# Gating one matrix's loads out of a shared weight ring, with planning margins, in a recurrent attention and mixer kernel

## The chip, the cores and the metric

The kernel runs on one core of one Trainium2 chip. The metric is the device time of one execution in microseconds (us). The executions of one kernel in one session spread by 7 to 28 us, so nearly every kernel was timed in five rounds beside the kernel before, on the same chip. Each run has one profile, of one of its executions, so differences of a few us between two profiles are noise.

Engines: TensorE (PE in the profile, its weight loads PEld), VectorE (DVE), ScalarE (ACT), GpSimd (POOL), SyncE (SP). SP and POOL both issue DMA transfers here. In the views, `psq`, `psk`, `psv` and `psy` are attention's q, k, v and output products, `psh` and `y` the mixer's (`y` is the one with w4), and `wst` is a slot of the weight ring.

## The reference, cut to what matters

```python
# four layers: attention with recurrent memory, mixer, attention, mixer
x = x + A(layernorm(x)); x = x + B(layernorm(x)); x = x + A(layernorm(x)); x = x + B(layernorm(x))

def A(x, mem0, Wq, Wk, Wv, Wo, seg_len):      # S = 2048, Dm = 640, 32 heads of 192, segments of 32
    mem = mem0                                # 8 memory rows
    for s in range(64):
        h = concat([mem, x[segment s]])       # 40 rows
        q, k, v = h @ Wq, h @ Wk, h @ Wv      # each 640 x 6144
        o = softmax(mask(q k^T) * scale) v @ Wo
        mem = o[:8]; outs.append(o[8:])       # the next segment needs this segment's memory rows

def B(x, w1, w2, w3, w4):                     # w1, w2: 640 x 640; w3: 640 x 1536; w4: 1536 x 640
    h = gelu(layernorm(x) @ w1); x1 = x + shift(h) @ w2
    return x1 + gelu(layernorm(x1) @ w3) @ w4
```

(Keyword details, the mask and the shift are left out.)

The recurrence makes attention a chain of 64 segments. Each one needs all of Wq, Wk, Wv and Wo again, 31 MB, not all of which is kept on the chip.

## The kernel before

Both attention layers run at once as two lanes, the second five segments behind the first, so that one pass over the weights serves both (80 columns in a full step, 40 where only one lane runs). There are 69 steps (48 us long in the model, eight groups of heads). After every second step a mixer chunk of 128 rows is worked off beside the next two steps.

About 60% of the attention weights stay resident. The rest comes through a ring of 16 slots, which the mixer's weights share. SP issues attention's loads, POOL the mixer's. Each queue is sorted by a "due" time and issued in that order. Cuts are marked by `...`:

```python
RING = 16; RING_A = 14; RING_B = 5         # slots; most that attention / the mixer may hold
...
plan = Plan({**PSUM_BANKS, "r": RING}, {**PSUM_USES, "ra": ("r", RING_A), "rb": ("r", RING_B)})
...
def block(t, kind, g, c, due):             # one streamed block of an attention weight
    ...
    b = ring("ra")
    def fn(op):
        return nc.sync.dma_start(out=T(b)[:, 0:n], in_=w_src(kind, g, c, c + 1)[:, 0, :])
    add("SP", SP_US, due, fn, w=(b,), dma=P * n * 2, queue="wa")
...
def load_b(c, nm, n, due):                 # one block of a mixer weight
    ...
    b = ring("rb")
    ...
    add("SP" if B_SP else "POOL", SP_US if B_SP else POOL_US, due, fn, w=(b,), dma=P * wd * 2, queue="wb")
```

A small simulator inside the kernel (`Plan.place`) plays all operations through a model of the engines and of the transfers, before the program is built. What it yields is the order of the instructions on each engine. At run time every engine works through its instructions in that order. If data come later than the model thought, the engine stands (below, TensorE for 1.24 us at one such place), whatever stands further down its list.

```python
if o.dma:
    srv = max(s + DMA_LAT, srv) + o.dma / DMA_RATE    # when the model thinks the data are there
    done = srv + DMA_SKEW
...
    b.free_at = max(b.free_at, done + LAT)            # when the slot can be filled again
...
for x in o.succ:
    if o.dma:
        at = done                                     # when the reader may be placed
```

In a step (48 us long in the model, eight groups of heads), `v` of the last group is due at 45.6, and the output weights of all groups are held back to the step's end, from 44 on:

```python
proj_v(g + 1, base + sl * (g + 1.6))        # last group: base + 6 * 7.6 = base + 45.6
...
held = g >= NG - OT_BUFS + 1                # true for all groups here
at = base + STEP - HOLD + 0.5 * g if held else ...     # HOLD = 4: base + 44, 44.5, 45, 45.5, 46, ...
ws = [block(t, "o", g, c, at + 0.03 * c) for c in range(GC)]
```

Of the kernel before, what the change touches and what calls it, by code (L numbers as in the profile page):

```python
# [20 lines left out]
LAG = 5  # L21
HG = 4
RING = 16
RING_A = 14
RING_B = 5
B_SP = False
POOL_US = 0.9
SP_US = 0.47
CUT = {"k": [3] * 8, "q": [3] * 8, "v": [3] * 8, "o": [2] + [4] * 7}
YA = 3  # L30
STEP = 48.0
# [10 lines left out]
LAT = 0.2  # L42
# [3 lines left out]
DMA_LAT = 2.2  # L46
DMA_SKEW = 2.0
FLIGHT = 10


class Buf:
# [34 lines left out]
class Plan:  # L86
# [48 lines left out]
    def place(self):  # L135
        in_queue = {}
        head = {}
        for q, lst in self.queues.items():
            lst.sort(key=lambda o: (o.due, o.i))
            for k, o in enumerate(lst):  # L140
                in_queue[o.i] = (q, k)
            head[q] = 0
        engines = sorted({o.e for o in self.ops})
        cand = {e: [] for e in engines}
        free = dict.fromkeys(engines, 0.0)
        waiting = {}

        def offer(o):
            if o.i in in_queue:
                q, k = in_queue[o.i]  # L150
                if k != head[q]:
                    waiting[o.i] = o
                    return
            cand[o.e].append(o)

        for o in self.ops:
            if o.n == 0:
                offer(o)
        left = len(self.ops)
        srv = 0.0  # L160
        landed = []
        out = []

        def est(o, t):
            s = max(t, o.ready)
            if o.dma and o.e == "SP" and len(landed) >= FLIGHT:
                s = max(s, landed[-FLIGHT])
            need = {}
            for b in o.slots:
                if b.slot is None:  # L170
                    need[b.cls] = need.get(b.cls, 0) + 1
            for c, n in need.items():
                fs = self.free_slots[self.pool_of[c]]
                al = self.allowed[c]
                if len(fs) < n or len(al) < n:
                    return None
                s = max(s, fs[n - 1][0], al[n - 1])
            return s

        while left:  # L180
            best = None
            for e in engines:
                t = free[e]
                lst = cand[e]
                if not lst:
                    continue
                vals = []
                m = None
                for o in lst:
                    s = est(o, t)  # L190
                    if s is not None:
                        vals.append((s, o))
                        if m is None or s < m:
                            m = s
                if m is None:
                    continue
                if best is not None and m >= best[0]:
                    continue
                lim = m + (LOOK if e == "PE" else 0.05)
                s, o = min((so for so in vals if so[0] <= lim), key=lambda so: (so[1].due, so[1].i))  # L200
                if best is None or s < best[0]:
                    best = (s, o)
            assert best is not None, "no operation can be placed"
            s, o = best
            e = o.e
            for b in o.slots:
                if b.slot is None:
                    b.slot = self.free_slots[self.pool_of[b.cls]].pop(0)[1]
                    self.allowed[b.cls].pop(0)
            o.start = s  # L210
            o.end = s + o.d
            free[e] = o.end
            done = o.end
            if o.dma:
                srv = max(s + DMA_LAT, srv) + o.dma / DMA_RATE
                done = srv + DMA_SKEW
                if e == "SP":
                    landed.append(done)
            cand[e].remove(o)
            out.append(o)  # L220
            left -= 1
            for b in o.slots:
                b.left -= 1
                b.free_at = max(b.free_at, done + LAT)
                if b.left == 0:
                    bisect.insort(self.free_slots[self.pool_of[b.cls]], (b.free_at, b.slot))
                    bisect.insort(self.allowed[b.cls], b.free_at)
            for x in o.succ:
                if o.dma:
                    at = done  # L230
                elif x.e == e:
                    at = o.end
                else:
                    at = o.end + (PE_LAT if e == "PE" else LAT)
                if at > x.ready:
                    x.ready = at
                x.n -= 1
                if x.n == 0:
                    offer(x)
            if o.i in in_queue:  # L240
                q, k = in_queue[o.i]
                head[q] = k + 1
                lst = self.queues[q]
                if k + 1 < len(lst) and lst[k + 1].i in waiting:
                    x = waiting.pop(lst[k + 1].i)
                    cand[x.e].append(x)
        return out
# [3 lines left out]
def kernel(  # L251
# [16 lines left out]
    nc = tc.nc  # L268
    P = 128
# [191 lines left out]
            return Dm, w4_v[:, n, :]  # L461
        return Dm, B_w2[P * n:P * n + P, :]

    def load_b(c, nm, n, due):

        if c >= NCH - 2:
            return ahead[nm, n]
        b = ring("rb")
        wd, src = mixer_src(nm, n)

        def fn(op):
            return (nc.sync if B_SP else nc.gpsimd).dma_start(out=T(b)[:, 0:wd], in_=src)  # L472
        add("SP" if B_SP else "POOL", SP_US if B_SP else POOL_US, due, fn, w=(b,), dma=P * wd * 2, queue="wb")
        return b, lambda: T(b)[:, 0:wd]


# [6 lines left out]
        return r  # L483

    last = [()]

    def HX(t, kc):
        return [B("hT", t % 4, k) for k in ("x0", "mA" if kc < YA else "mB", "xa", "xb", "xc")]

    def attention_step(t):  # L490
# [11 lines left out]
        def proj_kq(g, s0):  # L502
            G = t * NG + g
            for kind, off in (("k", 0.0), ("q", 0.3 * sl)):
                pq = ps("P", [P, GC, NS], f32, "ps" + kind)
                now = []
                for kc in range(KC):
# [7 lines left out]
                                             start=pq.begin(), stop=True, skip_group_check=True)  # L515
                    now.append(add("PE", mm_us(N, k=GC), due, fn, r=(wb, *HX(t, kc)), a=(pq,), after=last[0]))
                last[0] = now
                if kind == "q":
                    q = qT[G % 2]

                    def fq(op, pq=pq, q=q):
                        nc.scalar.copy(out=q[:, :, 0:N], in_=T(pq)[:, :, 0:N])  # L522
                    add("ACT", act_us(GC * N), s0 + off, fq, r=(pq,), w=(B("qT", G % 2),))
                else:
                    k_ = kT[G % 2]

                    def fk(op, pq=pq, k_=k_):
                        p4 = T(pq)[:].rearrange("p (h c) n -> p h c n", h=2)
                        k4 = k_[:].rearrange("p (h c) n -> p h c n", h=2)
                        nc.vector.tensor_copy(out=k4[:, :, 0::3, 0:N], in_=p4[:, :, 0::2, 0:N])  # L530
                    add("DVE", dve_us(4 * N), s0 + off, fk, r=(pq,), w=(B("kT", G % 2, 0),))

                    def fk2(op, pq=pq, k_=k_):
                        p4 = T(pq)[:].rearrange("p (h c) n -> p h c n", h=2)
                        k4 = k_[:].rearrange("p (h c) n -> p h c n", h=2)
                        for hf in range(2):
                            nc.vector.tensor_tensor(out=k4[:, hf, 1:3, 0:N],
                                                    in0=p4[:, hf, 1:2, 0:N].to_broadcast([P, 2, N]),
                                                    in1=halves[:].unsqueeze(2).to_broadcast([P, 2, N]), op=ALU.mult)
                    add("DVE", 2 * dve_us(2 * N), s0 + off, fk2, r=(pq,), w=(B("kT", G % 2, 1),))  # L540
# [297 lines left out]
    def prefetch(c):  # L838

        base = (2 * c + 2) * STEP  # L840
        units = [(nm, n, w[0] + w[1] * n) for nm, k, w in (("w1", KC, W1), ("w2", KC, W2), ("w3", 2 * KC, W3), ("w4", FC, W4))
                 for n in range(k)]
        for i, (nm, n, at) in enumerate(units):
            b, tl = resident["kqv"[i // 3 % 3], i // 9]
            wd, src = mixer_src(nm, n)
            ub = Buf()

            def fn(op, tl=tl, i=i, wd=wd, src=src):
                return nc.gpsimd.dma_start(out=tl[:, i % 3, 0:wd], in_=src)
            add("POOL", POOL_US, base + at * 0.6 * STEP, fn, w=(ub,), a=(b,), dma=P * wd * 2, queue="wb")  # L850
            ahead[nm, n] = ub, lambda tl=tl, i=i, wd=wd: tl[:, i % 3, 0:wd]

    def x2_chunks(a, b):
# [3 lines left out]
    def chunk(c):  # L857
# [102 lines left out]
        pz = [ps("B", [P, 3, XB], f32, "psh") for _ in range(2)]  # L960
        for kc in range(KC):
            due = D(W1[0] + W1[1] * kc)
            wb, wv = load_b(c, "w1", kc, due)

            def fw(op, kc=kc, wv=wv, pz=pz):
                w = wv()
# [150 lines left out]
    for t in range(T_A):  # L1117
# [3 lines left out]
        attention_step(t)  # L1121
        for _ in mixer:
            pass
        if c is not None:
            chunk_end(c)
    for c in range((T_A - 2 + 1) // 2, NCH):
        for _ in chunk(c):
            pass
        chunk_end(c)
    placed = plan.place()  # L1130
    ctx.enter_context(tc.manual_schedule())
    flight = []
# [43 lines left out]
```

## Time and profile before

| | before |
|---|---|
| median of three runs | 3533.4 us (3530.5 to 3536.1) |
| TensorE busy, weight loads busy | 96%, 92% |
| transfers | 1089 MB, 308 GB/s |
| a steady pair of steps, mean of 30 | 100.1 us |
| first step, and last step with the last chunk | about 99 us, 88.5 us |

The second line says that there is little room: TensorE is nearly always busy.

### The profile page before, as it was taken

How to read it: one execution, taken by the hardware profiler on the slowest of the kernel's cores; microseconds unless marked ns; L12 is line 12 of the kernel's file. 1: busy time of each engine (PE TensorE's matmuls, PEld its weight loads, DVE VectorE, ACT ScalarE, POOL GpSimd, SP SyncE). 2: the span in 40 equal slices, each digit the busy share in tenths (PEclk: the TensorE clock that was granted, in tenths of full speed). 3: DMA queues.
4: the chain of work that ended last, by engine and by line, in shares of the span. 5: the costliest groups of instructions: out<-in, count | busy, mean ns of one | idle time of the engine just before them, and what ended most of it. 6: DMA issues, size and time to landing. Idle time of an engine off the chain costs nothing.

```text
span 3534.4 us, 194661 instructions
## 1 busy us (share of the span) xinstructions
PE 3384.3 (96%) x84693; PEld 3257.0 (92%) x84693; DVE 2378.1 (67%) x7184; ACT 1714.3 (49%) x3583; POOL 883.9 (25%) x1581
## 2 busy tenths in 40 slices
PE   6899999999999999999999999999999999999897
PEld 4789999999999999999999999999999999999786
DVE  2456777777666777676677776766667777766455
ACT  2334555545554555454445554545455554554343
POOL 1022222222222222222222222222222222222222
PEclk9999999999999999999999999999999999999898
DMA  9999999999999999999999999999999999999995
GB/s 339 308 304 312 311 314 311 312 309 316 311 314 310 312 309 307 315 304 311 301 314 310 306 315 309 308 305 313 308 310 324 310 313 308 313 309 313 298 317 193
DMA packets 735258, 1089.24 MB, mean 308 GB/s; under 512 B 95358, under 2 KB 691596, under 8 KB 734400
## 3 DMA queue, kind: packets, MB, share of 16 engines
q1 hardware_dynamic: 669504, 874.19, 75.5%
q0 software_dynamic: 64896, 202.59, 17.1%
q8 instruction: 662, 10.85, 1.3%
q14 instruction: 196, 1.61, 0.1%
HBM read 1071.16 MB, written 5.24 MB: 305 GB/s over the span
## 4 chain that ended last, share of the span: by engine, by line
PE 80%; DMA 14%; issue 4%; DVE 1%; POOL 1%; ACT 0%; SPq 0%; POOLq 0%; DVEq 0%; ACTq 0%
PE psy L653 15%; PE psq L514 14%; PE psv L555 14%; PE psk L514 14%; DMA wst<-in_B_w_dram 5%; PE psvt L567 5%; PE pss L586 4%; PE pso L634 4%; PE psh L1025 3%; DMA wst<-in_A_Wv_dram 3%; DMA wst<-in_A_Wo_dram 2%; PE y L1047 2%; PE pst L619 2%; PE hs L994 1%; PE psh L968 1%
## 5 line engine op out<-in xcount | busy, mean ns | idle before, releaser
L472 POOL DMA_DIRECT2D wst<-in_B_w_dram x1056 | 581.7, 551 | 1690.5 <-PE psy L653 387.9
L640 DVE CAST oT<-pso 128x480 bf16<-128x480 f32 (+1 forms) x552 | 342.3, 620 | 413.6 <-PE pso L634 412.6
L571 ACT COPY V<-psvt 80x768 bf16<-80x768 bf16 (+1 forms) x552 | 439.3, 796 | 332.1 <-PE psvt L567 323.5
L514 PEld LDWEIGHTS <-wst 128*128 128x128 bf16 x13248 | 555.6, 100 | 31.2 <-issue 10.2
L653 PE MATMUL psy<-oT,wo 128*128 128x80 bf16 (+1 forms) x10350 | 511.0, 199 | 21.1 <-DMA wo<-in_A_Wo_dram 9.1
L522 ACT CAST qT<-psq 128x480 bf16<-128x480 f32 (+1 forms) x552 | 292.5, 530 | 441.7 <-PE psq L514 364.2
L555 PE MATMUL psv<-hT,wv 128*128 128x80 bf16 (+1 forms) x9936 | 477.8, 199 | 6.2 <-issue 3.5
L514 PE MATMUL psk<-hT,wk 128*128 128x80 bf16 (+1 forms) x9936 | 465.0, 199 | 5.6 <-issue 4.2
L514 PE MATMUL psq<-hT,wq 128*128 128x80 bf16 (+1 forms) x9936 | 454.7, 199 | 12.4 <-DMA wq<-in_A_Wq_dram 7.1
L561 ACT CAST vTs<-psv 128x480 bf16<-128x480 f32 (+1 forms) x552 | 292.1, 529 | 335.0 <-PE psv L555 325.0
L653 PEld LDWEIGHTS <-wo 128*128 128x128 bf16 x10350 | 423.0, 99 | 28.3 <-issue 12.5
L597 DVE CUSTOM_DVE_ANT_1 pss<-pss,mask 80x320 f32<-80x320 f32 (+1 forms) x512 | 245.8, 480 | 270.3 <-PE pss L586 228.5
L555 PEld LDWEIGHTS <-wv 128*128 128x128 bf16 x9936 | 405.3, 99 | 20.2 <-issue 4.3
L514 PEld LDWEIGHTS <-wk 128*128 128x128 bf16 x9936 | 399.7, 100 | 14.4 <-issue 6.5
L514 PEld LDWEIGHTS <-wq 128*128 128x128 bf16 x9936 | 393.6, 100 | 20.8 <-DMA wq<-in_A_Wq_dram 8.1
L514 PE MATMUL psk<-hT,wst 128*128 128x80 bf16 (+1 forms) x6624 | 352.9, 199 | 8.6 <-issue 8.0
L653 PE MATMUL psy<-oT,wst 128*128 128x80 bf16 (+1 forms) x6210 | 351.8, 199 | 8.8 <-DMA wst<-in_A_Wo_dram 4.7
L555 PE MATMUL psv<-hT,wst 128*128 128x80 bf16 (+1 forms) x6624 | 342.6, 199 | 12.4 <-DMA wst<-in_A_Wv_dram 9.2
L624 ACT COPY PT<-pst 80x320 bf16<-80x320 bf16 (+1 forms) x552 | 223.0, 404 | 261.6 <-PE pst L619 258.8
L514 PE MATMUL psq<-hT,wst 128*128 128x80 bf16 (+1 forms) x6624 | 326.2, 199 | 8.3 <-DMA wst<-in_A_Wq_dram 5.2
L604 ACT ACTIVATE pss<-pss,sm 80x320 f32<-80x320 f32 (+1 forms) x552 | 261.4, 474 | 137.4 <-DVE sm L597 137.3
L609 DVE TENSOR_REDUCE sm<-pss 80x4 f32<-80x320 f32 (+1 forms) x552 | 251.9, 456 | 92.5 <-ACT pss L604 91.7
(135 smaller groups left out, 5501.6 us busy)
## 6 DMA issues: line engine op xcount, KB each, us to landing
wst<-in_A_Wk_dram SPq DMA_DIRECT2D x1104, 192.0 KB, 4.7
wst<-in_A_Wq_dram SPq DMA_DIRECT2D x1104, 192.0 KB, 4.7
wst<-in_A_Wv_dram SPq DMA_DIRECT2D x1104, 192.0 KB, 4.8
wst<-in_A_Wo_dram SPq DMA_DIRECT2D x1242, 160.0 KB, 4.7
wst<-in_B_w_dram POOLq DMA_DIRECT2D x726, 160.0 KB, 5.0
wst<-in_B_w_dram POOLq DMA_DIRECT2D x330, 192.0 KB, 5.3
wk<-in_A_Wk_dram SPq DMA_DIRECT2D x8, 576.0 KB, 7.6
wq<-in_A_Wq_dram SPq DMA_DIRECT2D x8, 576.0 KB, 7.4
```

The source lines that it names most:

```text
L472: return (nc.sync if B_SP else nc.gpsimd).dma_start(out=T(b)[:, 0:wd], in_=src)
L514: nc.tensor.matmul(out=o[:, c, 0:N], lhsT=w[:, c * P:(c + 1) * P], rhs=h[:, kc, c0:c0 + N], start=pq.begin(), stop=True, skip_group_check= ...
L522: nc.scalar.copy(out=q[:, :, 0:N], in_=T(pq)[:, :, 0:N])
L555: nc.tensor.matmul(out=o[:, c, 0:N], lhsT=w[:, c * P:(c + 1) * P], rhs=h[:, kc, c0:c0 + N], start=pv.begin(), stop=True, skip_group_check= ...
L561: nc.scalar.copy(out=vs[:, :, 0:N], in_=T(pv)[:, :, 0:N])
L571: nc.scalar.copy(out=V_[0:N, :, 0:Dh], in_=T(pt)[0:N].rearrange("n c f -> n (c f)").rearrange("n (i e) -> n i e", i=HG))
L597: nc.vector.tensor_tensor_reduce(out=o, in0=o, in1=maskt.unsqueeze(1).to_broadcast([N, HG, N]), scale=-scale, scalar=3.0e38, op0=ALU.add, ...
L604: nc.scalar.activation(out=o, in_=o, func=ACT.Exp, bias=sm_[0:N, 0:1], scale=-1.0)
L609: nc.vector.reduce_sum(out=sm_[0:N, 4:4 + HG], in_=o, axis=AX.X)
L624: nc.scalar.copy(out=Pt[0:N, :, 0:N], in_=T(pst)[0:N, :, 0:N])
L640: nc.vector.tensor_copy(out=o_[:, :, 0:N], in_=T(pso)[:, :, 0:N])
L653: nc.tensor.matmul(out=T(psy[j])[:, m - m0, c0:c0 + N], lhsT=w[:, m * P:(m + 1) * P], rhs=o_[:, c, 0:N], start=psy[j].begin(), stop=True, ...
```

## The change

The intent: the five blocks of the mixer's first matrix (w1) shall not sit in the ring for half a pair before they are read; they wait for the end of the step ahead, and attention may use all 16 slots meanwhile. The plan gets margins for the mixer's loads. The weights of the last two chunks, which are loaded once and shared, go into SP's queue, in one order with attention's.

```diff
-RING_A = 14
+RING_A = 16
+B_SLACK = 1.5
+AH = 8.0
+B_FREE = 0.5
...
-                b.free_at = max(b.free_at, done + LAT)
+                b.free_at = max(b.free_at, done + (B_FREE if b.cls == "rb" else LAT))
...
-                    at = done
+                    at = done + (B_SLACK if o.e == "POOL" else 0.0)
...
+                mark[t, g] = now[:1]              # first matmul of group g's q in step t
...
-            wb, wv = load_b(c, "w1", kc, due)
+            wb, wv = load_b(c, "w1", kc, due, mark.get((2 * c + 1, NG - 1), ()))
...                                               # shared load of the last two chunks
-                return nc.gpsimd.dma_start(out=tl[:, i % 3, 0:wd], in_=src)
-            add("POOL", POOL_US, base + at * 0.6 * STEP, fn, w=(ub,), a=(b,), ..., queue="wb")
+                return nc.sync.dma_start(out=tl[:, i % 3, 0:wd], in_=src)
+            add("SP", SP_US, base + at * 0.6 * STEP + AH, fn, w=(ub,), a=(b,), ..., queue="wa")
```

(`load_b` passes the new argument on as `after`. Also, `chunk_end` is added to the plan one step later.)

More of the change, by code (lines that the diff above doesn't have):

```diff
@@ L462, in mixer_src, with load_b @@
         return Dm, B_w2[P * n:P * n + P, :]
-    def load_b(c, nm, n, due):
+    def load_b(c, nm, n, due, after=()):
         if c >= NCH - 2:
@@ L472, in fn @@
             return (nc.sync if B_SP else nc.gpsimd).dma_start(out=T(b)[:, 0:wd], in_=src)
-        add("SP" if B_SP else "POOL", SP_US if B_SP else POOL_US, due, fn, w=(b,), dma=P * wd * 2, queue="wb")
+        add("SP" if B_SP else "POOL", SP_US if B_SP else POOL_US, due, fn, w=(b,), dma=P * wd * 2, queue="wb", after=after)
         return b, lambda: T(b)[:, 0:wd]
@@ L485 @@
     last = [()]
+    mark = {}
     def HX(t, kc):
@@ L848, in fn @@
             def fn(op, tl=tl, i=i, wd=wd, src=src):
-                return nc.gpsimd.dma_start(out=tl[:, i % 3, 0:wd], in_=src)
-            add("POOL", POOL_US, base + at * 0.6 * STEP, fn, w=(ub,), a=(b,), dma=P * wd * 2, queue="wb")
+                return nc.sync.dma_start(out=tl[:, i % 3, 0:wd], in_=src)
+            add("SP", SP_US, base + at * 0.6 * STEP + AH, fn, w=(ub,), a=(b,), dma=P * wd * 2, queue="wa")
             ahead[nm, n] = ub, lambda tl=tl, i=i, wd=wd: tl[:, i % 3, 0:wd]
@@ L1123 @@
             pass
-        if c is not None:
-            chunk_end(c)
-    for c in range((T_A - 2 + 1) // 2, NCH):
-        for _ in chunk(c):
-            pass
-        chunk_end(c)
+        if t >= 3 and t % 2 == 1:
+            chunk_end((t - 3) // 2)
+    chunk_end(NCH - 2)
+    for _ in chunk(NCH - 1):
+        pass
+    chunk_end(NCH - 1)
     placed = plan.place()
```

## The prediction

> **What bounds the kernel now.** I read the page first, then the chain of waits, then busy time by stretch, the waits of TensorE, and last the timeline of the loads. From the page: the busy row of TensorE, two rows of the forty slices, and the head of the chain.
>
> ```profile
> PE 3384.3 (96%) x84693; PEld 3257.0 (92%) x84693; DVE 2378.1 (67%) x7184; ACT 1714.3 (49%) x3583; POOL 883.9 (25%) x1581
> ...
> PEclk9999999999999999999999999999999999999898
> ...
> GB/s 339 308 304 312 311 314 311 312 309 316 311 314 310 312 309 307 315 304 311 301 314 310 306 315 309 308 305 313 308 310 324 310 313 308 313 309 313 298 317 193
> ...
> PE 80%; DMA 14%; issue 4%; DVE 1%; POOL 1%; ACT 0%; SPq 0%; POOLq 0%; DVEq 0%; ACTq 0%
> ```
>
> TensorE is busy 96% of the span, weight loads 92%, and four fifths of the chain is TensorE: it is the first suspect. The rate of transfer is a flat 310 GB/s, which could be a second roof. Two stretches of the start, one steady pair of attention steps and the last step of the recurrence tell the two apart (columns: stretch, its length, busy time and count of each engine, granted clock, DMA share, GB/s).
>
> ```profile
> 20.00:60.00 40.00, 29.95 (x574) 23.88 (x575) 10.70 (x45) 10.88 (x26) 0.00 (x0) 1.00 1.07 373
> 100.00:140.00 40.00, 37.82 (x1157) 34.39 (x1154) 17.48 (x74) 17.47 (x42) 0.00 (x0) 1.00 0.94 303
> 1544.00:1644.00 100.00, 98.22 (x2458) 96.03 (x2455) 71.11 (x209) 51.20 (x104) 25.89 (x46) 1.00 0.95 309
> 3446.00:3504.00 58.00, 51.60 (x1270) 44.67 (x1266) 34.52 (x123) 22.48 (x55) 23.23 (x42) 0.88 0.88 293
> ```
>
> The first stretch shows that 373 GB/s is to be had. So 303 to 309 is not the transfer roof; it is what a ring of 16 slots gives when each slot waits for its reader, is filled, and waits again. For TensorE's own floor in a pair I take three entries of the chain:
>
> ```profile
> 1526.64 1.07 PE psq L514 x30
> ...
> 1555.54 0.84 PE psh L968 x15
> ...
> 1567.31 1.09 PE hs L994 x8
> ```
>
> That is 36 ns a matmul of 80 columns, 56 ns of 128 and 136 ns of 320. By the code one full step has 1056 matmuls of 80 columns (720 for q, k and v, 240 for the output, 64 and 32 in attention), 38 us; 48 transposes of 128 columns, 2.7; and 48 score matmuls at some 50 ns, 2.4. Two steps are 86 us. A mixer chunk adds 115 of 56 ns (6.4) and 34 of 136 ns (4.6). The pair's floor is 97 us, and it takes 100: only about 3% is left in a steady pair. At the edges, where only one lane runs, a step is well above its floor.
>
> **What the Trainium skill says.** "Perfetto Trace Analysis", section Optimization Strategy, says that consistent bubbles on an engine that should be saturated can mean that there is too little buffer for the next tile. The trace agrees in kind, but the steady bubbles are small (below). "DMA: Bandwidth & Descriptors", section Issuing engines are not separate DMA queues, says that transfers from all issuers share the same 16 engines and interleave, so that another issuer saves only issue time. The trace shows what that could save here: an issue by POOL takes 0.55 us, one by SP 0.33 to 0.38, and neither queue is full. The same page's Specifications give about 358 GB/s from HBM for a core; 373 was measured here, and the measurement decides. "TensorE: Matmul & The Clock Gate", section on the clock gate, has half rate after idle windows; the page's clock row stays at 9 until the last slices, and the pair above has 1.00, so in the steady part little is to be won there.
>
> **The change part by part.**
>
> 1. The first mixer weights (5 loads) wait for the first q matmul of the last group of the step ahead. Here is when they were issued before, and when they are first read; the first line is the last load of the preceding matrix:
>
> ```profile
> 1519.40 0.55 POOL L472 DMA_DIRECT2D wst<-in_B_w_dram  x1 [0.95 <-PE psq L514]
> 1521.17 0.55 POOL L472 DMA_DIRECT2D wst<-in_B_w_dram  x1 [1.23 <-DMA wst<-in_B_w_dram]
> 1522.52 0.55 POOL L472 DMA_DIRECT2D wst<-in_B_w_dram  x1 [0.80 <-PE y L1047]
> 1523.43 0.55 POOL L472 DMA_DIRECT2D wst<-in_B_w_dram  x1 [0.37 <-PE psk L514]
> 1524.84 0.55 POOL L472 DMA_DIRECT2D wst<-in_B_w_dram  x1 [0.86 <-PE psq L514]
> ...
> 1528.87 0.60 POOL L472 DMA_DIRECT2D wst<-in_B_w_dram  x1 [1.40 <-PE psv L555]
> ```
>
> They are read at 1554.8 to 1557. Their slots are thus held about 30 us of every 100. But the new gate opens at 1526.64 (the x30 of q above is the last group's). Four loads move by some 2 to 5.5 us, the fifth not at all: 15 slot-us out of the ring's 1600 per pair. A landing takes 5 us, so the loads are still there 20 us early. In a steady pair this part is nearly nothing, because the gate opens only when the old schedule had almost finished these loads.
>
> 2. In the start it is more. The first five were issued at 7 to 11 us, and POOL's next load of the ring is at 154 us: five slots lay full and unread through steps 0 and 1. Their 0.8 MB go out of the stretch that runs at 373 GB/s (2.2 us). Step 1 (99 to 142 us, 12.4 MB by the code, which at 303 GB/s is 41 us) ran with 11 slots. With 16 it could go toward 12.4 MB / 0.373 = 33 us; TensorE needs about 31 (25 ns for a matmul of 40 columns, x30 in 0.75 us in the chain). I take 5 us for both, as the w1 loads come back at the end of step 1.
>
> 3. RING_A from 14 to 16 matters only when the mixer holds fewer than two slots. It asks greedily and holds up to five in a steady pair, so attention has 11 and the old cap was hardly ever reached. Worth: 0 to 3 us in all, mainly between the last w4 read and the gate, and in the last step.
>
> 4. The margins: the plan, which fixes each engine's order, counts a POOL load as landed 1.5 us later, and a mixer slot as free 0.5 instead of 0.2 us after its reader. The rows they concern, from TensorE's waits between 250 and 3250 us (total, times, longest):
>
> ```profile
> PE y L1047 <- DMA wst<-in_B_w_dram: 14.6, 23, 1.9
> ...
> PE psy L653 <- DMA wst<-in_A_Wo_dram: 4.3, 8, 1.1
> PE psv L555 <- DMA wst<-in_A_Wv_dram: 1.5, 4, 0.6
> PE psq L514 <- DMA wst<-in_A_Wq_dram: 1.0, 2, 0.7
> ```
>
> The y waits are 23 of 0.6 us mean, longest 1.9, so a margin of 1.5 should cover most: 11 of the 14.6 us. The ring waits of attention sum to 6.8 us in the same stretch; parts 1 and 3 may take 2 of them.
>
> 5. The 32 shared loads of the last two chunks go from POOL to the SP queue, in one order with attention's, 8 us later. Attention should win and the mixer lose in 3446 to 3504; the bytes are the same. Step 68 ends at 3504 and the 30 us chain after it does not change. I take 2 us, between a gain of 8 and a loss of 5.
>
> 6. chunk_end is added to the plan a step later: the same dues, the same predecessors, only another tie-break. Nothing by itself.
>
> Sum: 5 + 2 + 11 + 2 + 2 = 22 us; 3533 - 22 = 3511 us.
>
> **The rivals.** First, that ring slots are the real limit and the freed ones let transfers go at 373 instead of 309 GB/s everywhere. For it: the rate. Against it: the steady pair is 3 us above its floor, so even perfect feeding gives 3 x 31 pairs, about 90 us, and the slots move by only 5 us in 100. It would give 3450 to 3480. Second, that the margins cost more than they save. Five slots with a cycle near 7 us (12 w4 loads in 17 us) would be planned at 8.8 us, the mixer would finish about 3 us later in the pair, and the normalised rows for the next step with it. Against it: y ends at 1524.6 and the next step starts near 1542, with only the short chain of normalisation between. It would give 3535 to 3560. Third, that the SP queue, served in order, holds attention's loads behind a shared load that waits for a resident tile's last reader: 5 to 10 us at the end, 3515 to 3525. Fourth, that the changed order of the whole plan is a fresh draw: pairs of one and the same plan take from 97.4 to 103.7 us, so a few us either way are luck.
>
> **Range and chances.** The gain is made of small terms that are each bounded by a row above, and a new plan may shift other waits by 10 to 15 us. Predicted 3511 us, 3488 to 3535 with 8 in 10. Over 2% faster means under 3464 us, 69 us less: this needs the first rival, 0.05. Over 2% slower means above 3605: 0.01. Within 2%: 0.94.
>
> **What would show it.** Right: no POOL load of the ring before about 125 us; step 1 shorter by 4 to 6 us and its rate above 330 GB/s; the wait of y on mixer weights under 5 us in total; the five w1 loads issued a few us later than before, in a burst after the last group's q; steady pairs near 99.5 us. Wrong: a steady rate well above 320 GB/s with pairs near 97 (first rival); y or the state copies later and a new wait of k or q at the step's start (second); SP waits on TensorE's last readers near 3450 us with attention starved (third).

## More of the kernel before

One view was not looked at closely enough when the prediction was written. It is the timeline of SP's loads at the end of an odd step (columns: start, length, engine, line, operation, names, count):

```profile
1519.35 0.80 SPq L448 DMA_DIRECT2D wst<-in_A_Wv_dram  x2
1521.33 7.00 SPq L448 DMA_DIRECT2D wst<-in_A_Wo_dram  x10
1528.82 2.12 SPq L448 DMA_DIRECT2D wst<-in_A_Wv_dram  x2
1531.03 5.15 SPq L448 DMA_DIRECT2D wst<-in_A_Wo_dram  x8
```

Here is the queue order. Ten output blocks take 7 us to issue (SP waits for a slot's last reader before seven of them, 5.6 us in all by its waits in 1521 to 1528.5), and only then come the last group's v blocks, although v is used before most of the output weights.

(The program also lets SP have at most ten transfers in flight. That did not hold SP up: wherever the traces tell the landings, 3820 loads (95 to 3400 us), the tenth load back had landed before SP's previous issue ended.)

## The result, and the profile after

The changed kernel took 3529.3 us (median of four runs, 3524.0 to 3534.0), against 3534.7 for the kernel before. The ratio was 0.9985, with a 95% interval of 0.9963 to 1.0007. A ratio is the mean time of one kernel's fast runs over the mean of the other's in the same rounds, so it is not quite the ratio of the medians. Repeated later in five rounds, it was 0.9964 (0.9948 to 0.9980; 3526.5 us). So the change is worth some 5 us, not clear of zero, by the first measurement and 12 by the second. "Within 2%" held and so did the range, but the predicted 22 us were not there.

From the page after:

```profile
PE 3372.2 (96%) x84693; PEld 3247.2 (92%) x84693; DVE 2372.7 (67%) x7184; ACT 1715.8 (49%) x3583; POOL 857.8 (24%) x1549
...
GB/s 339 312 320 312 313 301 316 315 307 314 315 313 315 314 314 308 308 310 309 315 314 315 301 309 319 306 317 312 312 311 319 308 318 306 311 315 315 319 308 162
```

The rate is as flat as before; no 373 GB/s appears beyond the start. The first rival is out. (The chain of waits can't be compared: in the trace after it breaks off at the end, with 0% everywhere.)

TensorE's waits in the window from 250 to 3230 us (who waited for what, total us, times, longest), first before, then after:

```profile
PE y L1047 <- DMA wst<-in_B_w_dram: 14.6, 23, 1.9
...
PE psv L555 <- DMA wst<-in_A_Wv_dram: 1.1, 3, 0.6
```

```profile
PE psv L560 <- DMA wst<-in_A_Wv_dram: 20.8, 28, 1.6
...
PE psq L518 <- DMA wst<-in_A_Wq_dram: 0.7, 1, 0.7
PE psy L658 <- DMA wst<-in_A_Wo_dram: 0.6, 2, 0.3
PE psvt L572 <- issue: 0.4, 2, 0.2
...
PE y L1052 <- issue: 0.2, 1, 0.2
```

This is the first finding. The wait of y on mixer weights, 14.6 us before, has gone entirely. In its place the wait of v on its streamed blocks has grown from 1.1 us to 20.8 us. It sits in one place of a step: 20 of the 28 waits come 88 to 91 us after the start of a pair, the other 8 about 40 us after it, in the even step. It is the v of a step's last group. SP's loads there:

```profile
1612.38 1.32 SPq L451 DMA_DIRECT2D wst<-in_A_Wv_dram  x2
1614.37 6.60 SPq L451 DMA_DIRECT2D wst<-in_A_Wo_dram  x10
1621.06 0.86 SPq L451 DMA_DIRECT2D wst<-in_A_Wv_dram  x2
1622.01 6.28 SPq L451 DMA_DIRECT2D wst<-in_A_Wo_dram  x8
```

The ten output blocks still take 6.6 us, with 16 slots allowed (3.0 us of it are waits for slots' readers), and TensorE's timeline at the same place shows what it waits for:

```profile
1624.59 0.46 PE L591 MATMUL pss<-kT,qT 128*80 128x80 bf16 x6
1626.28 0.39 PE L560 MATMUL psv<-hT,wst 128*128 128x80 bf16 x6 [1.24 <-DMA wst<-in_A_Wv_dram]
```

It stands for 1.24 us until the block issued behind the ten has landed.

The start was the second place. The same two stretches as in the prediction, after:

```profile
20.00:60.00 40.00, 28.95 (x557) 23.11 (x554) 10.55 (x45) 10.47 (x25) 0.00 (x0) 1.00 1.07 372
100.00:140.00 40.00, 36.87 (x1080) 32.78 (x1077) 16.70 (x71) 16.63 (x41) 2.77 (x5) 0.99 0.94 304
```

```profile
122.24 0.60 POOL L475 DMA_DIRECT2D wst<-in_B_w_dram  x1 [113.79 <-DMA wst<-in_A_Wk_dram]
```

The gate works as foreseen: POOL's first ring load comes at 122 us. But step 1 runs at 304 GB/s, as before, with five more slots, so these did not raise the rate. SP still waits for the readers of slots there (12.4 us of the 22 from 100 to 122, 9.1 before).

The end was the third. The last step of attention, and the last chunk after it, before and then after:

```profile
3445.90:3504.20 58.30, 51.75 (x1275) 44.84 (x1272) 34.70 (x124) 22.48 (x55) 23.33 (x42) 0.88 0.88 292
3504.20:3534.40 30.20, 13.46 (x134) 9.64 (x134) 14.37 (x45) 5.42 (x14) 2.50 (x3) 0.72 0.01 2
```

```profile
3426.40:3485.90 59.50, 53.33 (x1272) 45.13 (x1269) 33.89 (x122) 22.24 (x55) 5.02 (x9) 0.89 0.90 283
3485.90:3523.00 37.10, 13.75 (x136) 9.89 (x133) 15.16 (x46) 5.41 (x14) 3.01 (x4) 0.66 0.01 4
```

The last chunk has the same work, yet takes 6.9 us longer. The closing instructions of POOL (shortest, median and longest in ns) tell why; the kernel before comes first:

```profile
L1171 POOLq DRAIN  x3: 46/93/2716, 3530.9 to 3534.1; - x3
```

```profile
L1176 POOLq DRAIN  x3: 46/93/9069, 3513.1 to 3522.7; - x3
```

The last store was issued at 3513.1 us in the changed kernel and landed at 3515.0; POOL's DRAIN ran on to 3522.2.

Put together from the starts of the chunks in the two profiled runs (one run each, so a few us are noise):

| stretch | before | after | difference |
|---|---|---|---|
| to the first chunk | 141.7 | 142.1 | +0.4 |
| first pair, one lane | 102.7 | 98.5 | -4.2 |
| 30 pairs | 3003.3 | 2990.9 | -12.4 |
| next pair, one lane from there on | 104.3 | 98.0 | -6.3 |
| next pair | 93.9 | 96.9 | +3.0 |
| last step | 58.2 | 59.5 | +1.3 |
| last chunk to the end | 30.3 | 37.1 | +6.8 |
| span | 3534.4 | 3523.0 | -11.4 |

### The profile page after: what moved, and what is told of

Its sections match the earlier page's. It is cut to its first block, busy times and chain, and to the rows that moved or that the text cites. A ratio compares the mean times of both kernels' runs of the same rounds, so it can differ in the third digit from the quotient of the medians.

```text
span 3523.0 us, 194519 instructions
## 1 busy us (share of the span) xinstructions
PE 3372.2 (96%) x84693; PEld 3247.2 (92%) x84693; DVE 2372.7 (67%) x7184; ACT 1715.8 (49%) x3583; POOL 857.8 (24%) x1549
## 5 line engine op out<-in xcount | busy, mean ns | idle before, releaser
L475 POOL DMA_DIRECT2D wst<-in_B_w_dram x1056 | 574.3, 544 | 1991.1 <-PE psh L1030 631.0
L518 PEld LDWEIGHTS <-wst 128*128 128x128 bf16 x13248 | 550.7, 100 | 27.7 <-issue 7.2
L658 PE MATMUL psy<-oT,wo 128*128 128x80 bf16 (+1 forms) x10350 | 498.8, 199 | 13.6 <-DMA wo<-in_A_Wo_dram 7.7
L518 PE MATMUL psq<-hT,wq 128*128 128x80 bf16 (+1 forms) x9936 | 463.4, 199 | 15.3 <-DMA wq<-in_A_Wq_dram 9.4
L560 PE MATMUL psv<-hT,wv 128*128 128x80 bf16 (+1 forms) x9936 | 468.9, 199 | 6.5 <-issue 3.3
L560 PEld LDWEIGHTS <-wv 128*128 128x128 bf16 x9936 | 397.4, 99 | 15.4 <-issue 4.8
L518 PE MATMUL psk<-hT,wst 128*128 128x80 bf16 (+1 forms) x6624 | 343.7, 199 | 6.9 <-issue 3.9
L560 PEld LDWEIGHTS <-wst 128*128 128x128 bf16 x6624 | 279.4, 99 | 38.0 <-DMA wst<-in_A_Wv_dram 32.6
```

The source lines that it names most:

```text
L475: return (nc.sync if B_SP else nc.gpsimd).dma_start(out=T(b)[:, 0:wd], in_=src)
L518: nc.tensor.matmul(out=o[:, c, 0:N], lhsT=w[:, c * P:(c + 1) * P], rhs=h[:, kc, c0:c0 + N], start=pq.begin(), stop=True, skip_group_check= ...
L560: nc.tensor.matmul(out=o[:, c, 0:N], lhsT=w[:, c * P:(c + 1) * P], rhs=h[:, kc, c0:c0 + N], start=pv.begin(), stop=True, skip_group_check= ...
L658: nc.tensor.matmul(out=T(psy[j])[:, m - m0, c0:c0 + N], lhsT=w[:, m * P:(m + 1) * P], rhs=o_[:, c, 0:N], start=psy[j].begin(), stop=True, ...
```

## The experiments

All kernels gave correct results. The theories: A, the new wait of v comes from the order and pace of the loads at a step's end and shows as soon as y's wait is gone; B, the gate makes it, because w1's five loads now fall into that very place. C came later: the plan is too hopeful about attention's loads. The four parts of this section ran in the same rounds; the changed kernel itself was not in them.

### One part at a time

**The margins alone** on the kernel before.

```diff
+B_SLACK = 1.5
+B_FREE = 0.5
```

> The kernel before with the two planning margins alone (POOL loads counted 1.5 us later, mixer slots free after 0.5 us). Theory A (the waits of y move to the last group's v, because the loads of the step's end arrive no earlier): TensorE's wait of y on mixer weights, 14.6 us before, falls under 2 us, its wait of psv on the v weights rises from 1.5 to over 8 us in the steady part, and the time stays within 10 us of before (ratio 0.997 to 1.000). Theory B (the gate makes the wait of v): y's wait goes, psv's stays under 4 us, and the time falls by 12 us or more (ratio under 0.9965).

Measured: 3516.5 us, ratio 0.9958 (0.9938 to 0.9979), 14 us in the means. The y row is gone:

```profile
PE psv L557 <- DMA wst<-in_A_Wv_dram: 6.0, 12, 2.1
...
PE psy L655 <- DMA wst<-in_A_Wo_dram: 5.3, 10, 1.2
```

Alone, this part won at least as much as the whole change (5 and 12 us). The wait of v grew by 5 us, less than A said, and the time fell by more. The prediction's 11 us for this part were about right.

**The gate and RING_A 16** on the kernel before.

```diff
-RING_A = 14
+RING_A = 16
+... mark.get((2 * c + 1, NG - 1), ())
```

> The kernel before with the gate on the first mixer weights and RING_A 16, without the margins and with the shared load as before. Theory A: y's wait stays near 14 us, psv's wait stays under 8 us, ratio 0.998 to 1.001. Theory B: psv's wait on v weights comes to 15 us or more although y's is still there, so the kernel is no faster or slower than before (1.000 to 1.004). In both the start gains under 3 us, as the w1 loads come back at the end of step 1.

Measured: 3536.7 us, ratio 1.0013 (0.9989 to 1.0037): nothing, or slightly slower.

```profile
PE y L1049 <- DMA wst<-in_B_w_dram: 10.6, 21, 1.2
...
PE psv L557 <- DMA wst<-in_A_Wv_dram: 7.1, 10, 1.8
```

So both parts bring on the wait of v, and neither theory has it right alone: 6.0 us with the margins, 7.1 with gate and ring, 20.8 with all.

**The shared load alone** on SP, on the kernel before.

> The kernel before with the shared load alone on the SP queue, 8 us later. If the loss of the end seen in the changed kernel's profile (the last two stages 88.5 to 96.6 us) is due to this part: the time from the transposes of the last but one chunk to the end is 3 to 9 us above 88.5, the rest as before, ratio 1.001 to 1.0025. If it is due to the new plan in general: within 2 us of 88.5 and a ratio of 1.000.

Measured: 3546.5 us, ratio 1.0038 (1.0015 to 1.0061), 14 us slower. The last step and chunk took 60.4 and 37.1 us, 9 more than the 88.5 before, and POOL's last DRAIN 8.8 us. This part costs, and more than expected.

**The changed kernel without the gate.**

```diff
-            wb, wv = load_b(c, "w1", kc, due, mark.get((2 * c + 1, NG - 1), ()))
+            wb, wv = load_b(c, "w1", kc, due)
```

> The changed kernel without the gate (RING_A 16, margins, shared load kept). Theory A: psv's wait on v weights stays above 10 us in the steady part, time within 5 us of the changed kernel (ratio to before 0.997 to 1.000). Theory B: the wait falls under 5 us and the kernel is 10 us or more faster than the changed one (ratio under 0.9965).

Measured: 3520.5 us, ratio 0.9961 (0.9938 to 0.9984), v waiting 13.0 us. As A said, the wait stays. The changed kernel has 0.9985 and 0.9964 in other rounds, so within the intervals the gate is worth nothing in it.

Where v's loads and v's matmuls meet, taken from the traces as medians of the pairs (us after the start of the pair, odd steps; the landing is known in about half of the pairs):

| kernel | v loads issued | second landed | second block used | wait of v |
|---|---|---|---|---|
| before | 85.5 | 91.1 | 92.5 | 1.1 |
| margins alone | 85.1 | 91.0 | 91.2 | 6.0 |
| gate and RING_A 16 | 83.5 | 88.8 | 88.7 | 7.1 |
| changed | 83.5 | 89.5 | 89.4 | 20.8 |

The gate does help attention: its v blocks land some 2 us earlier. But the plan, which knows of the freed slots, puts their use 3 to 4 us earlier, right onto the landing. The margins do the same from the other side: v is used 1.3 us earlier, while its blocks land as late as before. (The 1.1 us of before is for the window to 3230 us; the prediction's 1.5 is to 3250.)

### The queue order, and three rivals of it

**The last group's v blocks ahead of the output blocks**, nothing else, on the changed kernel:

```diff
-                wb, wv = block(t, "v", g, kc, due)
+                wb, wv = block(t, "v", g, kc, due - (2.0 if g == NG - 1 else 0.0))
```

> The changed kernel with one due changed: the v weights of a step's last group stand in the load queue ahead of the ten output weights, no longer behind them. Theory A (queue order and the rate of the load stream at the step's end set the new wait): the second v load of the odd step lands 5 us or more earlier than 89.5 us after the pair's start, psv's wait on v weights in the steady part falls from 20.8 to under 5 us, psy's wait on output weights rises to 3 to 15 us, and the time falls by 0 to 12 us against the changed kernel. Theory C (the plan's order on TensorE is too hopeful about attention's loads, whichever comes last): the wait moves whole to psy, the sum stays 15 us or more, no gain.

Measured: 3509.2 us, ratio 0.9909 (0.9890 to 0.9929). SP's queue now reads

```profile
1613.03 3.17 SPq L451 DMA_DIRECT2D wst<-in_A_Wv_dram  x4
1616.29 11.13 SPq L451 DMA_DIRECT2D wst<-in_A_Wo_dram  x18
```

and TensorE's waits

```profile
PE psy L658 <- DMA wst<-in_A_Wo_dram: 5.2, 6, 1.8
```

with 0.6 us for v. The second v block lands at 82.6 instead of 89.5. It is the strongest single edit: the three other variants of the changed kernel in these rounds have means of 3527.5 to 3528.3 us, this one 3508.2, so 19 us, more than the 12 that had been the upper end. The changed kernel itself was not in these rounds.

**A margin of 0.8 us on SP's loads too** (theory C), on the changed kernel.

```diff
+A_SLACK = 0.8
...
-                    at = done + (B_SLACK if o.e == "POOL" else 0.0)
+                    at = done + (B_SLACK if o.e == "POOL" else A_SLACK)
```

> The changed kernel with a planning margin of 0.8 us on the SP loads too. Theory C: the sum of TensorE's waits on ring loads of attention falls from 22 to under 8 us in the steady part and the kernel gains 8 to 15 us on the changed one. Theory A: the loads arrive no earlier, TensorE meets them in another order, and the waits stay above 12 us.

Measured: 3526.8 us, ratio 0.9966 (0.9945 to 0.9987). The waits fell to 8.2 us, almost as C said:

```profile
PE psv L561 <- DMA wst<-in_A_Wv_dram: 4.5, 7, 0.9
PE psy L659 <- DMA wst<-in_A_Wo_dram: 3.1, 4, 1.2
```

but the time did not, as far as other rounds tell: the changed kernel has 0.9964 in its own repeat. The second v block lands at 89.7 us, no earlier than in the changed kernel. Here a wait that was planned away was not time won.

**A later gate**, at the last output matmul of the step ahead, on the changed kernel.

```diff
-mark.get((2 * c + 1, NG - 1), ())
+mark.get((2 * c + 1, "o"), ())
```

(The new mark is set where that matmul is added to the plan.)

> The changed kernel with the gate of the first mixer weights at the last output matmul of the step ahead, so that attention has all 16 slots through the step's end. If the five slots and the transfers of those loads are what delays attention there: the last output load is issued 1 us or more earlier than 90.3 us after the pair's start, ring waits of attention fall under 10 us in the steady part, 5 to 15 us faster than the changed kernel. If the loads at the next step's start only shift: psk, psq or psh L9xx waits of 5 us or more appear and the time stays.

Measured: 3529.8 us, ratio 0.9973 (0.9950 to 0.9995). The last output block is issued at 89.1 instead of 90.3 and v waits 11.6 us instead of 20.8, but there is no gain beyond the spread.

**The very last store issued by SP**, on the changed kernel, to see what the DRAIN hangs on.

```diff
-                nc.gpsimd.dma_start(out=dst[w0 + a:w0 + b, :], in_=xo[2 * a + lane:2 * b:2, :])
+                return (nc.sync if c == NCH - 1 else nc.gpsimd).dma_start(...)
...
```

(In the plan this store counts for SP accordingly.)

> The changed kernel with only the very last store issued by SP instead of POOL. The three kernels with the shared load on SP ended with a DRAIN of POOL of 8.8 to 9.1 us after its last store, those without with 2.7 us. If the drain follows POOL's last transfer: it now starts before the last chunk is done, is hidden, and the last stage falls from 37.1 to 30 to 31 us, ratio 0.0015 to 0.002 lower than the changed kernel's. If it is due to something else at the end: the last stage stays above 36 us.

Measured: 3526.4 us, ratio 0.9964 (0.9941 to 0.9987). The DRAIN is as long as ever, 9.6 us, but starts at 3507.4 us and ends before the kernel does:

```profile
L1176 POOLq DRAIN  x3: 46/98/9577, 3507.4 to 3523.3; - x3
```

The last chunk takes 30.9 us. So 6 of the 14 us of the shared load on SP are this DRAIN at the very end. In the ratio 6 us are too few to be seen.

### Putting parts together

The next four ran in the same rounds. **The changed kernel again:**

> The changed kernel itself once more, in the same rounds as the next three, so that they can be set against it: ratio to before 0.996 to 1.000, the wait of psv on v weights 12 to 25 us in the steady part, POOL's last DRAIN near 9 us.

Measured: 3526.5 us, ratio 0.9964 (0.9948 to 0.9980), v waiting 24.5 us, DRAIN 9.1 us.

**The changed kernel with v ahead and the shared load back on POOL:**

> The changed kernel with the last group's v loads ahead of the output weights and with the shared load back on POOL's queue. If the parts add: the 0.9909 of the run with the v loads ahead, less the 6 to 13 us that the shared load on SP cost alone: 0.987 to 0.9905, with POOL's last DRAIN back at 2.7 us. If the SP order of the shared load helped the last step of attention: 0.991 or more.

Measured: 3503.1 us, ratio 0.9894 (0.9877 to 0.9912), DRAIN 2.7 us.

**With v ahead and the last store on SP, the shared load left on SP:**

> The changed kernel with the v loads ahead and the last store on SP; the shared load stays on SP. If only the drain made the shared load on SP costly: as fast as the run before this or faster, 0.987 to 0.990, last stage near 31 us. If the later mixer in the last step costs as well: 2 to 6 us slower than the run before this.

Measured: 3503.5 us, ratio 0.9898 (0.9882 to 0.9914). The two are equal; once the drain is hidden, the issuer of the shared load no longer shows.

**The kernel before with the margins and v ahead**, without gate, RING_A 16 and shared load on SP:

> The kernel before with the margins and the v loads ahead, without gate, RING_A 16 and shared load on SP. If gate and RING_A 16 give attention something once the queue order is right: 4 us or more slower than the run with the v loads ahead and the shared load on POOL. If they give nothing: within 4 us of it.

Measured: 3513.8 us, ratio 0.9937 (0.9918 to 0.9956). So gate and RING_A 16, with the moved `chunk_end`, are worth 15 us in the means (3516.2 to 3501.1) once the v blocks stand ahead; gate and RING_A 16 alone had been worth nothing without that. Against the margins alone (0.9958, in other rounds) the v order gave only some 7 us here, less than the 19 above.

### What was still open

**With the last eight and with the first eight of the 32 shared loads on POOL:**

> The changed kernel with the last eight of the 32 shared loads on POOL. If the long DRAIN comes from POOL having issued little shortly before the end: 2.7 us again. If it comes from the number of POOL's transfers in the last step at large: near 9 us, or between.

> The changed kernel with the first eight of the shared loads on POOL. Recent issues matter: near 9 us, as in the changed kernel. Numbers matter: the same as in the run with the last eight.

Measured: 3532.8 and 3529.5 us (one run each, state unknown), and a DRAIN of 9.7 us in both. It does not matter which eight. But the "last eight" were issued from 3448 to 3454, more than 60 us before the end, so this did not test recent issues well. Over all profiles the DRAIN is 2.7 us where POOL issued 1314 transfers (nine profiles) and 8.8 to 9.7 us where it issued 1281, 1282 or 1290 (eleven profiles). Those with 1314 also have 9 or more of them in the last 60 us, the others 1 or 2. What the DRAIN waits for stays open.

**v ahead on the kernel before, alone:**

> The kernel before with the v loads of a step's last group ahead of the output weights, nothing else. If the change uncovered the queue order as the next bound: y's wait stays over 10 us, psv's was only 1 us, so the time is within 6 us of before (0.998 to 1.001). If the order was a bound of its own: ratio under 0.997.

Measured: 3524.4 us, ratio 0.9950 (0.9929 to 0.9970).

```profile
PE y L1047 <- DMA wst<-in_B_w_dram: 12.1, 21, 1.6
...
PE psv L555 <- DMA wst<-in_A_Wv_dram: 1.6, 1, 1.6
```

My idea that the change had uncovered the queue order falls: the order was a bound before it, with y's wait of 12.1 us still in place. The kernel before had only 6.7 us of visible waits on attention's ring loads in this stretch and gave 17 us. The two profiles show where: in their 30 steady pairs, 3003.3 and 2983.1 us long, TensorE's listed waits of all kinds fell by only 6.5 us, and its busy time by 12 (2945 to 2934) for the same matmuls. A matmul counts as busy for some 200 ns on the page while the next can start 36 ns after it, so a stand shorter than the difference is inside "busy" and in no wait row. What those short stands waited for is not shown.

**The best version with the later gate:**

> The best version so far (changed kernel, v loads ahead, shared load on POOL) with the gate at the last output matmul of the step ahead. Waits of attention on ring loads are only 3 us there, so there is little to win: within 5 us of it, ratio 0.988 to 0.991. If slots still bind at the step's end: under 0.988. If the mixer's weights come too late: psh waits at the chunk's start and over 0.991.

Measured: 3518.9 us, ratio 0.9925 (0.9904 to 0.9946). This missed: it is slower than the best version's 0.9894. The waits on ring loads rose from 2.6 to 8.0 us, spread over v, q, k and the output; the five w1 blocks now go out from 97.6 to 102.8 us, among the first loads of the next step (82.9 to 91.7 in the best version). No wait of the mixer's first matmuls appeared.

**The best version without the gate, and the best version again beside it:**

> The best version (margins, RING_A 16, gate, v loads ahead, shared load on POOL) without the gate. If the gate makes the 15 us: 8 us or more slower than the best version in the same rounds, and the last output load of the odd step is issued near 91.8 us after the pair's start as in the version with the margins alone, not 89.0. If RING_A 16 makes them: within 4 us of the best version.

> The best version again, as the reference of the run before: ratio 0.988 to 0.991, the waits of attention on ring loads under 5 us in the steady part, POOL's last DRAIN 2.7 us.

Measured: without the gate 3514.3 us, 0.9919 (0.9900 to 0.9938); the best version 3500.2 us, 0.9883 (0.9863 to 0.9903). The last output block of the odd step is issued at 91.2 us without and 89.3 us with the gate. So the gate itself is worth 11 us in the means (3512.4 to 3501.0). RING_A 16 and the moved `chunk_end` together are left with some 4 to 6 us, within the intervals (0.9937 without both, 0.9919 with). Part of the gate's gain lies where one lane runs: the pair after the 30 steady ones took 102.8 us in the mean of the seven profiles without a gate and 99.3 us in the eleven with this one. In the 30 steady pairs themselves the profiles show no gain: 2971.6 us without the gate, 2964.4 and 2975.6 us in the two profiles of the best version. With one execution each, which spread by 7 to 18 us, where the rest comes from stays open.

The best version is thus the changed kernel with v ahead and the shared load on POOL: 37 and 42 us (1.1 and 1.2%) faster than the kernel before in its two sessions, 25 us faster than the changed one in common rounds (3526.2 to 3501.1).

## Why the prediction was right or wrong

**What bounds the kernel: right.** Little was to be had in a steady pair (99.7 us after the change, 98.8 and 99.2 in the best version, 97 estimated as the floor), the rate stayed near 310 GB/s, and no version reached 2%. That 303 to 309 GB/s "is what a ring of 16 slots gives" is not shown: five more slots in step 1 left it at 304, and the stretch with 373 moved resident blocks of 576 KB among others, where step 1 moves blocks of 160 and 192 KB.

**Where the 22 us went.** By the table of stretches, the start took 0.4 us more instead of 5 less (part 2), and the last step and chunk took 8.1 us more instead of 2 less (part 5). The 30 pairs gave 12.4 us (8.3 in the profile of the repeat) of the 15 that the other parts promised; that this is near is partly luck, as the margins' gain met a loss that the prediction did not have. The two pairs with one lane gave 10.5 us that no term had, and the pair after them lost 3.

**Part 4, the margins alone: right in the row and about right in size.** 11 us predicted, 14 measured alone, and y's row empty. The second rival, that the margins cost more than they save, did not come true. In the whole change much of this gain was taken back by v's wait, which is the next point.

**The step that failed in the steady pairs: "The ring waits of attention sum to 6.8 us in the same stretch; parts 1 and 3 may take 2 of them."** It took the visible waits as all that hung on attention's loads, and had no term for a wait that would take the place of y's. There was one: v's wait went up by 20 us. The view that shows it was in the trace before, the ten output blocks ahead of the two v blocks. The visible wait was small there only because the plan had put v's use behind the landing. An edit of that order alone gave 17 us to the kernel before, two and a half times what its wait rows allowed. Here a wait row was no upper bound: the planner had moved the work to where the data are, and short stands are in no row.

**Parts 1 and 3, the gate: "nearly nothing" in a steady pair: right as measured alone (1.0013), but mis-sized in its working.** The five loads were to move by 0 to 5.5 us, 15 slot-us together; by medians they moved by 6 to 10 us each (first 77.4 to 83.3, last 85.5 to 91.4 after the pair's start), 39 slot-us together, because they go out 1 to 4 us apart after the gate, where one issue takes 0.55 us. The gate brings v's blocks in 2 us earlier. It is worth nothing measurable without the new queue order and 11 us with it, but the steady pairs of the profiles do not show this gain.

**Part 2, the start: wrong.** "With 16 it could go toward 12.4 MB / 0.373 = 33 us" assumed that step 1 was held by its slots. With the slots given, the rate stayed at 304 GB/s and the first chunk began at 142.1 instead of 141.7 us (139.7 in the repeat). Step 0 did win what it should: step 1 began at 96.2 instead of 99.1 us. But step 1 then took 43.2 us instead of 40.2 and ended where it had (counted from its first k matmul to that of step 2). The visible waits on ring loads there are small, 1.4 us against 0.7. The w1 loads came back just where the output weights are loaded, from 122 to 130 us, as the prediction had said; that they cost the 3 us is argued, not tested.

**Part 5, the shared load: wrong in sign, outside its own bounds.** Predicted a gain of 2, at worst a loss of 5; alone it cost 14 us. 6 us of this are POOL's DRAIN, which no step of the prediction had ("the 30 us chain after it does not change": it took 37.1 instead of 30.3, and 30.9 with the last store on SP). The rest is not settled: in its one profile the last step was 2 us longer, and the version that hides the drain is as fast as the one that keeps the load on POOL. The third rival (attention starved at the end) did not come true: in the changed kernel attention's last output matmul came 54.5 us after the step's chunk began, 57.9 before. What came last was the mixer's y, up to 59.4.

**The sum, then.** 22 us predicted; the parts measured alone give -14 for the margins, +5.5 for gate and ring (within noise), +14 for the shared load, about +6 together. The whole measured -5 and -12, so the parts miss it by 11 to 18 us. Part of this can be noise, and part the moved `chunk_end`, never tested alone. Every edit also re-orders the whole plan, and the prediction's fourth rival said that this is a fresh draw. No run re-plans without a purpose, so how much of any one gain is luck of the draw is not known; for the v order, the sign was the same on the kernel before, with the margins and on the changed kernel (17, 7 and 19 us).

## What to carry to other kernels

Where a planner fixes the order of each engine, read the order of the load queue against the order of use, not only the waits: a small wait can mean that the planner has parked the work behind a late load. Here freeing buffers gave nothing measurable until the load needed next stood ahead in the queue. Measure the parts of such a change one by one; here one part lost what another won, and the best version kept three of them (and the moved `chunk_end`) and added one line.

## What the Trainium skill lacked or had wrong

- No page that I read tells of a closing DRAIN of GpSimd whose length differs with its DMA issues (why, stays open): 2.7 us at the end with 1314 transfers issued, 8.8 to 9.7 us with 1281 to 1290, running on seven us after the last store had landed. It would belong to "DMA: Bandwidth & Descriptors", whose section Issuing engines are not separate DMA queues says only that another issuer saves issue time: here the move of 32 loads from POOL to SP cost 14 us, 6 of them by that DRAIN.
- "Perfetto Trace Analysis", section Optimization Strategy, offers too few buffers as a possible reason for consistent bubbles. The consistent bubble here (v, 28 times in the steady part, 20.8 us) stayed with all 16 slots allowed and went to 0.6 us when two loads changed place in the queue. Queue order should stand beside buffer count there.
